# A recurrent attention with streamed weights: side transfers on another issuing engine, an output product in a bank of its own, key loads in portions, and three streaming places for 11 blocks

## The chip, the cores and the metric

The kernel runs on one core of one Trainium2 chip. The metric is the device time of one execution in microseconds, as the median of several runs; lower is better. The profile is of one further execution, and its spans are counted from its first instruction.

## The reference

Two independent computations whose outputs stand side by side.

A is a recurrent attention. The sequence of 2048 rows is cut into 64 segments of 32 rows. Each segment is put behind 8 memory rows, and the first 8 rows of its result are the memory of the next:

```python
for s in range(n_seg):                        # 64, one after the other
    xs = x[:, s * seg_len:(s + 1) * seg_len, :].copy()
    h = jnp.concatenate([mem, xs], axis=1)    # 8 + 32 rows of 1024
    q = jnp.einsum('btd,dhe->bhte', h, Wq)    # 32 heads of 128; k and v alike
    ...
    scores = jnp.where(mask[None, None], scores, -1000000000.0)
    p = _softmax(scores, axis=-1)
    o = jnp.einsum('bhqk,bhke->bhqe', p, v)
    o = jnp.einsum('bhte,hed->btd', o, Wo)
    mem = o[:, :M, :].copy()
    outs.append(o[:, M:, :])
```

B is a long convolution: from complex parameters a kernel K of 1024 channels by 2048 steps, which is convolved with u by Fourier transforms, plus `u * Dskip`.

## The kernel before

**Order of the whole.** Part B runs first (`part_b`, from line 639), part A after it (`part_a`, from line 233). Work of A that doesn't hang on the memory (projections of the last 8 rows of each segment, line 115) is woven into B. The order of the instructions on each engine is that of the program, written by hand; a tile's dependencies become semaphore waits. SyncE issues nearly all transfers, in the order of the program: one that waits holds up all behind it.

**B's end: spectra.** The loop on lines 1301 to 1345 has 16 passes, b = 0 to 15: four quarters of the channels, four blocks of frequencies each. In pass b, TensorE makes the spectrum of the keys for pass b + 1 (line 1039), VectorE multiplies pass b's with that of u (`pointwise`, lines 1210 to 1224; the first multiply by u is line 1218), and SyncE loads u's for pass b + 2 (`load_u`, two transfers on line 1013). From b = 4 on two inverse transforms follow in each pass (`inverses`). In pass 0, line 1306 issues the key loads of the third and fourth quarter: `load_k` (line 978) makes 31 small transfers for a quarter, all on SyncE. They are used from pass 7 on, and negated on ScalarE at the end of pass 6 (line 1336). In passes 0 to 3 SyncE also loads eight inverse matrices (line 1325), and weights of A where room has come free (`residents`, from line 1408).

**A's loop: segments.** All weights of A are cut into blocks of 128 x 2048 (512 KB): eight for each of k, q and v in two halves t of the heads, and 16 of the output projection. Here k1.4 is block 4 of k in half 1, and o11 the output's block 11. Most blocks stay in SBUF. Three are kept in PSUM, as bits (`KEPT`: k0.7, q0.7 or half of it, half of o15), and come into SBUF in each segment by `fetch` (line 311, copies on VectorE, line 292). Twelve are streamed from DRAM in each segment. `unit(key)` returns a block; for a streamed one `stage` (line 294) issues its load into the next of four places in turn (`SLOTS`). As SyncE runs ahead of TensorE, a load goes out when TensorE has done with the block that was in its place, four streamed blocks before.

A segment runs on TensorE as k0, q0, k1, q1, v0, v1 (`quads`: eight blocks each, four matmuls of 32 x 512 a block, line 364), with transposes (line 375), scores (lines 389 and 393) and products (lines 433 and 437) between them, and then the 16 blocks of the output projection (`oproj`, line 463). k0 is transposed by way of the copies KT0 (VectorE) and q0 by way of QT0 (ScalarE, line 483).

**Side transfers**, all on SyncE: `load_pk` (128 KB, the last rows' keys and queries of the segment, line 327), `load_vx` (their values and the next rows of x, 112 KB, line 333) and `stores` (two of 64 KB, lines 343 and 347, for the segment before). They are hung in front of the load of a certain streamed block by `between`. Small tiles of a segment lie by hand in one arena (`AT`, byte offsets), so a load waits until what was at its place has been read.

**A segment's end** (lines 565 to 577). The projection ends in bank b3, in the half `pp[:, 1]`. VectorE copies its left half out (line 568), ScalarE then the right half (line 569). The product of the last rows with half 1 (`pv_l`: four matmuls with V1 and one with the rows' own values) goes to `pp[:, 0]`, in the same bank b3, behind them. Then two transposes (line 574) and a copy on VectorE (line 575) put the memory rows into hT, which the next segment's first matmul waits for. The last segment also has GpSimd sort results for the closing output projection (line 603).

Of the kernel before, what the change touches and what calls it, by code (L numbers as in the profile page):

```python
# [21 lines left out]

STREAM = {("k", 0): (0, 6), ("q", 0): (3,), ("k", 1): (2,), ("q", 1): (0, 5), ("v", 0): (3, 7), ("v", 1): (4,)}
STREAM_O = (1, 7, 12)

BANK = {("k", 0): "b0", ("q", 0): "b1", ("k", 1): "b2", ("q", 1): "b0", ("v", 0): "b3", ("v", 1): "b2"}
KEPT = {("k", 0, 7): (("K7a", 0, 512), ("K7b", 512, 512), ("K7c", 1024, 512), ("K7d", 1536, 384), (None, 1920, 128)),
        ("q", 0, 7): (("Q7a", 1024, 512), ("Q7b", 1536, 512)),  # L30
        ("o", 15): (("Oa", 1024, 512), ("Ob", 1536, 384), (None, 1920, 128))}
HALF = (("q", 0, 7), ("o", 15))
SLOTS = 4

ARENA = 5984
AT = {"K7a": 2048, "K7b": 4960, "K7c": 0, "K7d": 3168, "ob": 1024, "pk": 3936, "vx": 0, "Q7a": 4960, "Q7b": 0, "k0": 2048,
# [196 lines left out]
def part_a(ctx, tc, x, src, WD, HE, seg_len, out_a, ahead, W_res, rest, places, first):  # L233
# [66 lines left out]
    def load_kept(key):  # L300
        t_ = first.pop(key) if key in first else stage(key, src(key))
        kept[key] = {}
        for n in (1,) if key in HALF else (0, 1):
            kept[key][n] = ps_k.tile([128, 512], F32, name="keep", tag="keep%d" % sum(len(b) for b in kept.values()))
            words(kept[key][n][:], t_[:, 1024 * n:1024 * n + 1024])
        if key in HALF:
            t_ = ahead.low["half"] if key[0] == "q" else wres.tile([128, 1024], BF16, name="Whalf")
            nc.sync.dma_start(out=t_[:], in_=src(key)[:, 0, :] if key[0] == "o" else src(key)[:, 0:1024])
            halves[key] = [(0, 1024, t_)]
# [14 lines left out]

    def load_pk(j):
        pk = at("pk", 512)
        nc.sync.dma_start(out=pk, in_=PKd[j])
        return pk

    def load_vx(j):  # L330
        n = 448 if j + 1 < NS else 256
        vx = at("vx", 448)
        nc.sync.dma_start(out=vx[:, 0:n], in_=VXd[j + 1, :, 0:n])
        return vx

    def put_xt(vx):
# [3 lines left out]
        return ap.to_broadcast(shape)  # L340

    def stores(s, ob):
        nc.sync.dma_start(out=OLd[s // 8][:, 256 * (s % 8):256 * (s % 8) + 256], in_=ob[:, 1, :])
        rows = out_a[s * SL:s * SL + SL, :].rearrange("r (q d) -> q r d", q=4)
        if s + 1 < NS:

            nc.sync.dma_start(out=rows, in_=ob[:, 0, :])
        else:
            for q in range(4):
                nc.sync.dma_start(out=rows[q][0:XM], in_=ob[32 * q:32 * q + XM, 0, :])  # L350

    load_kept(("k", 0, 7))
    fetch(("k", 0, 7))
    between["q", 0, 3] = lambda: load_kept(("q", 0, 7))
    between["v", 0, 3] = lambda: load_kept(("o", 15))
    for s in range(NS):
        def quads(m, t, kcs, a=None):
            if a is None:
# [69 lines left out]
            spread_l(nc.gpsimd, L[:, 1], lt[:, 4, 0:XL], 0, 16, XL)  # L428
            return L

        def pv(p, t, V, pb, lbs, first=True):
            for hl in range(4):
                nc.tensor.matmul(p[:, hl, :], lhsT=V[:, 128 * hl:128 * hl + 128], rhs=pb[:, hl, :],  # L433
                                 start=(first and hl == 0), stop=False, skip_group_check=True)
            p, lo = p.rearrange("p a b -> p (a b)"), 0
            for lb in lbs:
                nc.tensor.matmul(p[:, lo:lo + lb.shape[1]], lhsT=vl[:, t, :], rhs=lb,  # L437
                                 start=False, stop=True, skip_group_check=True)
                lo += lb.shape[1]
# [9 lines left out]
            nc.scalar.copy(out=o, in_=p[:].rearrange("p a (g q) -> p a g q", g=4))  # L449
            return o  # L450

        def pv_l(pl_, t, V, L):

            pv(pl_[:, t], t, V, L[:, 0].rearrange("p (a b) k -> p a (b k)", a=4), [L[:, 1].rearrange("p a k -> p (a k)")], first=(t == 0))

        def oproj(po, us, oT):
            for u in us:
# [5 lines left out]
                            nc.tensor.matmul(po[32 * qt:32 * qt + 32, o_:o_ + rhs.shape[1]], lhsT=oT[:, h % 4, (h % 16) // 4, :], rhs=rhs,  # L463
                                             start=False, stop=(h == 31), tile_position=(0, 32 * qt), skip_group_check=True)

        pks, vxs = [], []
        between["k", 1, 2] = lambda: pks.append(load_pk(s))
        if s:
            between["q", 1, 0] = lambda: stores(s - 1, ob)
        between["v", 0, 7] = lambda: vxs.append(load_vx(s))  # L470
        a = quads("k", 0, range(KC))
        k0 = evac(a, "k0")
        a = quads("q", 0, range(0, 6))
# [3 lines left out]
        sc0 = new_sc("b1")  # L477
        a = quads("k", 1, range(0, 3))
        pq, pk_ = (ps.tile([128, 4, 4, SL], BF16, name="tr", tag=tag) for tag in ("b0", "b3"))
        tr(q0, pq)  # L480
        tr(k0, pk_)
        QT0, KT0 = at("QT0", 4, 4, SL), at("KT0", 4, 4, NK)
        nc.scalar.copy(out=QT0, in_=pq[:])
        nc.vector.tensor_copy(out=KT0[:, :, :, 0:SL], in_=pk_[:])  # L484
        quads("k", 1, range(3, 6), a)
        pk = pks[0]
        kl, ql = ([pk[:, 256 * t + o:256 * t + o + 128].rearrange("p (a g k) -> p a g k", a=4, g=4) for t in range(2)] for o in (0, 128))
        put_kl(KT0, 0)
        scores(0, sc0, QT0, KT0)
# [47 lines left out]
        powers(sc1, 0)  # L537
        highest(sc1, 1)
        a = quads("v", 1, range(0, 4))
        vx = vxs[0]  # L540
        vl = vx[:, 0:256].rearrange("p (t e) -> p t e", t=2)
        pv0 = pv_x(0, V0, pb0, lb0)
        pp = ps.tile([128, 2, 256], F32, name="pp", tag="b3")
        pl_ = pp[:, 0, :].rearrange("p (t a k) -> p t a k", t=2, a=4)
        pv_l(pl_, 0, V0, L0)
        o0 = evac_o(pv0, "o0")
        pt1 = norm(sc1, 0, "pn1", "pt1")
        pb1 = at("pb1", 4, 4, SL)
# [16 lines left out]
        oproj(pp[:, 1, :], range(8, 16), o1)  # L565
        ob = at("ob", 2, 256)
        osb = ob[:, 0, :]
        nc.vector.tensor_copy(out=osb[:, 0:128], in_=pp[:, 1, 0:128])
        nc.scalar.copy(out=osb[:, 128:256], in_=pp[:, 1, 128:256])  # L569
        pv_l(pl_, 1, V1, L1)  # L570
        if s + 1 < NS:
            pt_o = ps.tile([128, 2, 4, SL], BF16, name="tro", tag="b2")
            for j in range(2):
                nc.tensor.transpose(out=pt_o[:, j, :, :].rearrange("p a b -> p (a b)"), in_=osb[:, 128 * j:128 * j + 128], identity=ident[:])
            nc.vector.tensor_copy(out=hT[:, :, XM:SL].rearrange("p (q j) r -> p j q r", j=2), in_=pt_o[:, :, :, XM:SL])
            fetch(("k", 0, 7))
        nc.scalar.copy(out=ob[:, 1, :], in_=pp[:, 0, :])

    order = sorted(range(16), key=lambda u: ("o", u) not in W_res)
    wo = {}  # L580
# [58 lines left out]
def part_b(ctx, tc, u, A_re, A_im, B_re, B_im, C_re, C_im, log_dt, Dskip, out_b, ahead, copies, residents, first_state):  # L639
# [335 lines left out]
                    at += n  # L975
            put(Kd[640:641, dsl], kx[P0:P0 + 1, NC - 1, :])

    def load_k(d0, n_d, qs, KT):
        dsl = slice(d0, d0 + n_d)

        def rows(r0, n, step=1):
            return Kd[r0:r0 + step * (n - 1) + 1:step, dsl]
        n_q = [0]

        def get(out, in_):
            qs[n_q[0] % len(qs)].dma_start(out=out, in_=in_)
            n_q[0] += 1
        for r in (0, 2, 1, 3):
            k0 = KT[:, 4 * r, :]
            get(k0[0:64], rows(r, 64, 4))  # L990
            get(k0[64:128], rows(256 + (0, 0, 1, 2)[r], 64, 2))
            k1 = KT[:, 4 * r + 1, :]
            if r == 2:
                get(k1[0:128:2], rows(384, 64, 2))
                get(k1[1:128:2], rows(386, 64, 2))
            else:
                get(k1[:], rows(384 + (0, 0, 0, 1)[r], 128))
            for mc in (2, 3):
                k2 = KT[:, 4 * r + mc, :]
                q0 = 512 + 64 * (mc - 2)  # L1000
                get(k2[0:128:2], rows(q0, 64))
                if r == 0:
                    get(k2[1:128:4], rows(q0, 32, 2))
                    get(k2[3:128:4], rows(q0 + 2, 32, 2))
                else:
                    get(k2[1:128:2], rows(q0 + 1, 64))
        return KT
# [266 lines left out]
    def inverse(dq, c, uu, neg, mn):  # L1274
# [14 lines left out]
        v.tensor_tensor(out=uu[:], in0=uu[:], in1=yb[:].rearrange("p b t s e -> p b (t s e)"), op=ALU.add)  # L1289
        gp.dma_start(out=out_v[r][:, mc:mc + 2, d], in_=uu[:])  # L1290

    todo = [(dq, c) for dq in range(4) for c in range(0, 16, 2)]
    nxt = []
    Bs = [None] * 4
# [6 lines left out]
    for b in range(16):  # L1301
        dq = b // 4
        if b % 4 == 0:
            Bs[dq] = (bp0, bp)[dq % 2].tile([128, 4, 2, 2, 2, DQ], BF16, name="Bt", tag="B")
        if b == 0:
            ks += [load_k(DQ * i, DQ, (sy,), KT2[i - 2]) for i in (2, 3)]
        if b == 3:
            nxt = [load_inverse(*todo[n_]) for n_ in range(NIV)]
            pointwise(b, *now)
            ctx_h.close()  # L1310
            ctx_p.close()
            ps_h = ctx.enter_context(tc.tile_pool(name="b_psh", bufs=3, space=PSUM))
            ps_y = ctx.enter_context(tc.tile_pool(name="b_psy", bufs=2, space=PSUM))
        if b + 1 < 16:
            s_ = [ps_h.tile([128, 2, 2, DQ], F32, name="hps", tag="h") for _ in range(2)]
            spectrum(b + 1, [halves(t_) for t_ in s_])
            then = s_[0][:], odd([halves(t_) for t_ in s_])
        if b != 3:
            pointwise(b, *now)
        now = then  # L1320
        if b + 2 < 16:
            spectra.append(load_u(b + 2))
        if b < 4:
            for i in (2 * b, 2 * b + 1):
                sy.dma_start(out=MI[i][:], in_=MId[2 * i:2 * i + 2].rearrange("c p a k q -> p c a k q"))
        for _ in range({1: 1, 2: 1, 3: 1, 6: 4, 11: 2, 12: 2, 13: 4, 14: 4}.get(b, 0)):
            next(resident)
        if b == 4:
            state = first_state(iv.tile([8, D], BF16, name="m0", bufs=1), iv.tile([128, 8, 24], BF16, name="xt0", bufs=1))
            next(state)  # L1330
        if b == 13:
            state.send(ps_y.tile([128, 8, 128], BF16, name="yp", tag="yp")[:, :, 0:8])
        if b >= 4:
            inverses(2)
        if b == 6:
            negate(ks[1:])
# [166 lines left out]
```

## Time and profile before

| | |
|---|---|
| median of 3 runs (lowest, highest) | 2226.33 us (2224.5, 2230.53) |
| profiled execution, time | 2218.38 us |
| its span | 2216.7 us |
| mean granted TensorE clock | 0.972 |
| busy: TensorE, its weight loads | 85%, 53% |
| busy: VectorE, ScalarE, GpSimd | 67%, 47%, 18% |
| DMA moved, mean over the span | 590.82 MB, 267 GB/s |
| line 577, one a segment: first and last start | 810.8 and 2156.9 us |

A line of the page's slices has forty digits, each the busy share of one fortieth of the span in tenths. Lines of a timeline give start, duration, engine, source line, operation, tiles as written <- read, shape and number, and in brackets the idle time before the first of them with what ended it. Lines of the waits give who waited for whom, the total in us, how often, and the longest. SPq is SyncE's issuing of transfers.

### The profile page before, as it was taken

To read this page: it belongs to the slowest core of one execution; us is meant where nothing else is said; L and a number is where in the kernel's file an instruction comes from. 1 tells how busy PE (TensorE), PEld (TensorE's weight loads), DVE (VectorE), ACT (ScalarE), POOL (GpSimd) and SP (SyncE) were. 2 spreads that over 40 slices of the span, in tenths; PEclk is the share of its full clock that TensorE was granted. 3 is DMA by queue.
4 is the path that set the end of the run, shared out by engine and by line. 5 is a ranking of instruction groups with operands and counts; after the bars stand their busy time and mean duration, and the time that the engine had idled before them with its cause. 6 is when DMAs were issued, how large, how long until landed. Compare 5 with 4: busy or idle time off the path is not lost.

```text
span 2216.7 us, 79278 instructions
## 1 busy us (share of the span) xinstructions
PE 1874.8 (85%) x33734; PEld 1176.4 (53%) x33734; DVE 1475.7 (67%) x3800; ACT 1041.7 (47%) x1855; POOL 404.5 (18%) x786
## 2 busy tenths in 40 slices
PE   1599999971999779898998898989989988998859
PEld 1365656651888535555555555545555455555434
DVE  8589999983999346665666666656656666666630
ACT  6699999940333224343443443443434434434420
POOL 2154453560011111111111111101111111111020
PEclk9999999976999879999999999999999999999989
DMA  6767787564536789999999999999999999999960
GB/s 160 203 193 237 213 217 201 154 167 158 194 119 209 268 321 326 308 324 316 318 327 315 324 328 311 323 319 315 329 313 321 323 313 325 325 324 325 317 247 28
DMA packets 344023, 590.82 MB, mean 267 GB/s; under 512 B 108537, under 2 KB 220185, under 8 KB 341621
## 3 DMA queue, kind: packets, MB, share of 16 engines
q1 hardware_dynamic: 331972, 547.87, 74.8%
q0 software_dynamic: 11696, 37.88, 4.9%
q8 instruction: 264, 4.33, 0.8%
q14 instruction: 91, 0.74, 0.1%
HBM read 530.86 MB, written 65.26 MB: 269 GB/s over the span
## 4 chain that ended last, share of the span: by engine, by line
PE 24%; DMA 19%; DVE 14%; issue 4%; ACT 2%; POOL 1%; SPq 0%; DVEq 0%; ACTq 0%; POOLq 0%
PE acc L364 11%; DMA wst<-WD_q 11%; PE pp L463 6%; DMA wst<-WD_v 5%; DVE arena L421 3%; PE pe L603 2%; DVE a_mx L398 2%; DVE arena L411 2%; DMA wst<-WD_k 2%; PE tr L375 1%; DVE a_mx L408 1%; ACT sc L404 1%; DVE arena L412 1%; DVE sc L401 1%; PE pv L437 1%
## 5 line engine op out<-in xcount | busy, mean ns | idle before, releaser
L364 PEld LDWEIGHTS <-a_hT 128*32 128x32 bf16 x12352 | 324.0, 96 | 378.0 <-issue 79.4
L370 ACT CAST arena<-acc 128x512 bf16<-128x512 f32 x384 | 225.3, 587 | 350.8 <-PE acc L364 296.2
L364 PE MATMUL acc<-W,a_hT 128*32 128x512 bf16 x4864 | 371.7, 382 | 0.0
L364 PE MATMUL acc<-wst,a_hT 128*32 128x512 bf16 x2304 | 231.3, 386 | 62.1 <-DMA wst<-WD_q 20.4
L463 PEld LDWEIGHTS <-arena 128*32 128x32 bf16 x8256 | 214.8, 97 | 80.4 <-issue 49.0
L292 DVE TENSOR_SCALAR arena<-keep 128x256 int32<-128x256 int32 (+1 forms) x512 | 175.6, 395 | 45.3 <-PE acc L364 41.5
L404 ACT ACTIVATE sc<-sc 128x160 f32<-128x160 f32 x256 | 73.7, 288 | 248.9 <-DVE sc L401 218.4
L463 PE MATMUL pp<-W_o,arena 128*32 128x256 bf16 x4608 | 174.2, 275 | 7.0 <-DMA W_o<-in_A_Wo_dram 6.7
L378 POOL COPY arena<-arena 128x128 bf16<-128x128 bf16 x128 | 39.1, 306 | 751.7 <-PE tr L375 462.0
L364 PE MATMUL acc<-MF,a_hT 128*32 128x512 bf16 x2048 | 158.4, 382 | 0.0
L398 DVE TENSOR_REDUCE a_mx<-sc 128x4 f32<-128x160 f32 x256 | 81.0, 316 | 109.6 <-ACT sc L404 56.0
L1039 PEld LDWEIGHTS <-MF 128*128 128x128 bf16 x1024 | 102.6, 100 | 64.3 <-issue 45.5
L1039 PE MATMUL hps<-KT,MF 128*128 128x256 bf16 x720 | 94.2, 283 | 48.7 <-DVE x L1214 45.7
L484 DVE COPY arena<-tr 128x512 bf16<-128x512 bf16 x64 | 27.2, 424 | 161.4 <-ACT sc L383 158.4
L433 PEld LDWEIGHTS <-arena 128*128 128x128 bf16 x1024 | 55.2, 97 | 138.9 <-ACT arena L569 61.6
L167 PE MATMUL pro<-xTl,wsl 128*128 128x512 bf16 x512 | 119.1, 383 | 5.2 <-ACT xTl L111 5.2
L426 POOL TENSOR_TENSOR arena<-arena,a_BD 128x128 bf16<-128x128 bf16 x128 | 51.0, 398 | 355.5 <-DVE arena L413 314.7
L408 DVE TENSOR_REDUCE a_mx<-sc 128x4 f32<-128x160 f32 x256 | 82.0, 320 | 50.4 <-ACT sc L404 50.4
L412 DVE STREAM_TRANSPOSE arena<-arena 128x128 bf16<-128x128 bf16 x256 | 79.8, 312 | 41.2 <-PE pp L433 19.5
L1271 PE MATMUL yp<-Bt,MI 128*128 128x256 bf16 x680 | 102.8, 273 | 0.8 <-ACT yb L1287 0.8
L1077 ACT ACTIVATE E<-pa 128x648 bf16<-128x648 f32 x128 | 91.3, 713 | 17.8 <-PE pa L1069 14.1
L433 PE MATMUL pp<-arena 128*128 128x32 bf16 x512 | 33.2, 178 | 75.1 <-ACT arena L569 50.5
(319 smaller groups left out, 4052.5 us busy)
## 6 DMA issues: line engine op xcount, KB each, us to landing
wst<-WD_k SPq DMA_DIRECT2D x192, 512.0 KB
wst<-WD_q SPq DMA_DIRECT2D x192, 512.0 KB
wst<-WD_v SPq DMA_DIRECT2D x192, 512.0 KB
wst<-WD_o SPq DMA_DIRECT2D x192, 512.0 KB
Ud<-ux POOLq DMA_DIRECT2D x16, 1024.0 KB, 6.2
uq<-Ud SPq DMA_DIRECT2D x32, 512.0 KB
wsl<-in_A_Wk_dram SPq DMA_DIRECT2D x16, 512.0 KB
wsl<-in_A_Wv_dram SPq DMA_DIRECT2D x16, 512.0 KB
```

Of the source, the lines that this page charges most:

```text
L167: nc.tensor.matmul(a[:], lhsT=w[:, kc, 128 * j:128 * j + 128], rhs=xTl[:, kc, :, :].rearrange("p s k -> p (s k)"), start=(kc == 0), stop=( ...
L292: nc.vector.tensor_scalar(out=out.bitcast(I32), in0=in_.bitcast(I32), scalar1=0, scalar2=None, op0=ALU.bitwise_or)
L364: nc.tensor.matmul(a[32 * g:32 * g + 32, o_:o_ + rhs.shape[1]], lhsT=hT[:, kc, :], rhs=rhs, start=(kc == 0), stop=(kc == KC - 1), tile_pos ...
L370: nc.scalar.copy(out=q, in_=a[:])
L398: nc.vector.tensor_reduce(out=mx[:, 4 * i:4 * i + 4], in_=sc[:, i], axis=AX.X, op=ALU.max)
L404: nc.scalar.activation(out=sc[:, i], in_=sc[:, i], func=ACT.Exp, scale=scale)
L408: nc.vector.tensor_reduce(out=m_, in_=sc[:, i], axis=AX.X, op=ALU.add)
L412: nc.vector.transpose(out=pt[:, 0:4, :], in_=pn[:, :, 0:SL])
L463: nc.tensor.matmul(po[32 * qt:32 * qt + 32, o_:o_ + rhs.shape[1]], lhsT=oT[:, h % 4, (h % 16) // 4, :], rhs=rhs, start=False, stop=(h == 3 ...
L1039: pe.matmul(s_[r][half][:, cs, :], lhsT=MF[:, kc, 4 * rr + mc, cs, :], rhs=rhs, start=(i == 0 and mc == 0), stop=(i == 1 and mc == 3), ski ...
L1077: sc.activation(out=T["E", r, e // 4][:, lo:lo + 8 * NE].rearrange("p (i c) -> p i c", i=2), in_=T.pop(("p", r, e))[:, :, 0:4 * NE], func= ...
L1271: pe.matmul(yp[:, b, :], lhsT=m_[:, b, cs, kc, :], rhs=Bt[:, kc, j, half, c_, :], start=(kc == 0 and cs == 0 and half == 0), stop=(kc == 3 ...
```

## The change

- Eleven blocks are streamed in place of twelve, through three places in place of four; the block no longer streamed is resident, in the room of the fourth place. Which blocks are streamed changes.
- The side transfers are issued by ScalarE, at fixed points of a segment: VX after QT0; PK of the next segment and both stores at the segment's end.
- At the end one ScalarE copy takes the whole projection out. The second half's product for the last rows gets a bank of its own (b2), and is split: four matmuls ahead of the transposes, one behind the copy into hT. The transposes go to bank b0. The fetch of k0.7 comes behind the fifth matmul.
- k0 is transposed ahead of q0.
- The key loads of the third and fourth quarter are put on a list, from which each pass issues ten, behind its load of u's spectra.

```diff
-STREAM = {("k", 0): (0, 6), ("q", 0): (3,), ("k", 1): (2,), ("q", 1): (0, 5), ("v", 0): (3, 7), ("v", 1): (4,)}
-STREAM_O = (1, 7, 12)
+STREAM = {("k", 0): (2, 5), ("k", 1): (0, 4), ("q", 1): (2,), ("v", 0): (1, 5), ("v", 1): (3, 6)}
+STREAM_O = (4, 11)
...
-SLOTS = 4
+SLOTS = 3
...
-        nc.sync.dma_start(out=pk, in_=PKd[j])
+        nc.scalar.dma_start(out=pk, in_=PKd[j])
...
-        nc.sync.dma_start(out=vx[:, 0:n], in_=VXd[j + 1, :, 0:n])
+        nc.scalar.dma_start(out=vx[:, 0:n], in_=VXd[j + 1, :, 0:n])
...
-        nc.sync.dma_start(out=OLd[s // 8][:, 256 * (s % 8):256 * (s % 8) + 256], in_=ob[:, 1, :])
+        nc.scalar.dma_start(out=OLd[s // 8][:, 256 * (s % 8):256 * (s % 8) + 256], in_=ob[:, 1, :])
...
-            nc.sync.dma_start(out=rows, in_=ob[:, 0, :])
+            nc.scalar.dma_start(out=rows, in_=ob[:, 0, :])
...
-    between["q", 0, 3] = lambda: load_kept(("q", 0, 7))
-    between["v", 0, 3] = lambda: load_kept(("o", 15))
+    pk = load_pk(0)
+    between["k", 0, 5] = lambda: load_kept(("q", 0, 7))
+    between["v", 0, 5] = lambda: load_kept(("o", 15))
...
-        def pv_l(pl_, t, V, L):
-
-            pv(pl_[:, t], t, V, L[:, 0].rearrange("p (a b) k -> p a (b k)", a=4), [L[:, 1].rearrange("p a k -> p (a k)")], first=(t == 0))
+        def pv_l(pl, t, V, L, parts=(0, 1)):
+
+            if 0 in parts:
+                pv(pl, t, V, L[:, 0].rearrange("p (a b) k -> p a (b k)", a=4), [])
+            if 1 in parts:
+                pv(pl, t, None, None, [L[:, 1].rearrange("p a k -> p (a k)")])
...
-        pks, vxs = [], []
-        between["k", 1, 2] = lambda: pks.append(load_pk(s))
-        if s:
-            between["q", 1, 0] = lambda: stores(s - 1, ob)
-        between["v", 0, 7] = lambda: vxs.append(load_vx(s))
...
+        tr(k0, pk_)
         tr(q0, pq)
-        tr(k0, pk_)
         QT0, KT0 = at("QT0", 4, 4, SL), at("KT0", 4, 4, NK)
         nc.scalar.copy(out=QT0, in_=pq[:])
+        vx = load_vx(s)
...
-        nc.vector.tensor_copy(out=osb[:, 0:128], in_=pp[:, 1, 0:128])
-        nc.scalar.copy(out=osb[:, 128:256], in_=pp[:, 1, 128:256])
-        pv_l(pl_, 1, V1, L1)
+        nc.scalar.copy(out=osb, in_=pp[:, 1, :])
+        pl = ps.tile([128, 4, 32], F32, name="pl", tag="b2")
+        pv_l(pl[:], 1, V1, L1, (0,))
         if s + 1 < NS:
-            pt_o = ps.tile([128, 2, 4, SL], BF16, name="tro", tag="b2")
+            pt_o = ps.tile([128, 2, 4, SL], BF16, name="tro", tag="b0")
             for j in range(2):
                 nc.tensor.transpose(out=pt_o[:, j, :, :].rearrange("p a b -> p (a b)"), in_=osb[:, 128 * j:128 * j + 128], identity=ident[:])
             nc.vector.tensor_copy(out=hT[:, :, XM:SL].rearrange("p (q j) r -> p j q r", j=2), in_=pt_o[:, :, :, XM:SL])
+        pv_l(pl[:], 1, V1, L1, (1,))
+        if s + 1 < NS:
             fetch(("k", 0, 7))
-        nc.scalar.copy(out=ob[:, 1, :], in_=pp[:, 0, :])
+        nc.scalar.copy(out=ob[:, 1, 0:128], in_=pp[:, 0, 0:128])
+        if s + 1 < NS:
+            pk = load_pk(s + 1)
+        nc.scalar.copy(out=ob[:, 1, 128:256], in_=pl[:].rearrange("p a k -> p (a k)"))
+        if s + 1 < NS:
+            stores(s, ob)
...
         def get(out, in_):
-            qs[n_q[0] % len(qs)].dma_start(out=out, in_=in_)
+            q = qs[n_q[0] % len(qs)]
             n_q[0] += 1
+            if later is None:
+                q.dma_start(out=out, in_=in_)
+            else:
+                later.append(lambda: q.dma_start(out=out, in_=in_))
...
-            ks += [load_k(DQ * i, DQ, (sy,), KT2[i - 2]) for i in (2, 3)]
+            ks += [load_k(DQ * i, DQ, (sy,), KT2[i - 2], keys) for i in (2, 3)]
...
         if b + 2 < 16:
             spectra.append(load_u(b + 2))
+        for _ in range(min(10, len(keys))):
+            keys.pop(0)()
```

More of the change, by code (lines that the diff above doesn't have):

```diff
@@ L342, in stores @@
     def stores(s, ob):
-        nc.sync.dma_start(out=OLd[s // 8][:, 256 * (s % 8):256 * (s % 8) + 256], in_=ob[:, 1, :])
+        nc.scalar.dma_start(out=OLd[s // 8][:, 256 * (s % 8):256 * (s % 8) + 256], in_=ob[:, 1, :])
         rows = out_a[s * SL:s * SL + SL, :].rearrange("r (q d) -> q r d", q=4)
         if s + 1 < NS:
-            nc.sync.dma_start(out=rows, in_=ob[:, 0, :])
+            nc.scalar.dma_start(out=rows, in_=ob[:, 0, :])
         else:
             for q in range(4):
-                nc.sync.dma_start(out=rows[q][0:XM], in_=ob[32 * q:32 * q + XM, 0, :])
+                nc.scalar.dma_start(out=rows[q][0:XM], in_=ob[32 * q:32 * q + XM, 0, :])
     load_kept(("k", 0, 7))
     fetch(("k", 0, 7))
-    between["q", 0, 3] = lambda: load_kept(("q", 0, 7))
-    between["v", 0, 3] = lambda: load_kept(("o", 15))
+    pk = load_pk(0)
+    between["k", 0, 5] = lambda: load_kept(("q", 0, 7))
+    between["v", 0, 5] = lambda: load_kept(("o", 15))
     for s in range(NS):
@@ L429, in left_blocks, with pv @@
             return L
-        def pv(p, t, V, pb, lbs, first=True):
-            for hl in range(4):
+        def pv(p, t, V, pb, lbs):
+            for hl in range(4 if V is not None else 0):
                 nc.tensor.matmul(p[:, hl, :], lhsT=V[:, 128 * hl:128 * hl + 128], rhs=pb[:, hl, :],
-                                 start=(first and hl == 0), stop=False, skip_group_check=True)
+                                 start=(hl == 0), stop=False, skip_group_check=True)
             p, lo = p.rearrange("p a b -> p (a b)"), 0
@@ L479, in part_a @@
         pq, pk_ = (ps.tile([128, 4, 4, SL], BF16, name="tr", tag=tag) for tag in ("b0", "b3"))
+        tr(k0, pk_)
         tr(q0, pq)
-        tr(k0, pk_)
         QT0, KT0 = at("QT0", 4, 4, SL), at("KT0", 4, 4, NK)
         nc.scalar.copy(out=QT0, in_=pq[:])
+        vx = load_vx(s)
         nc.vector.tensor_copy(out=KT0[:, :, :, 0:SL], in_=pk_[:])
         quads("k", 1, range(3, 6), a)
-        pk = pks[0]
         kl, ql = ([pk[:, 256 * t + o:256 * t + o + 128].rearrange("p (a g k) -> p a g k", a=4, g=4) for t in range(2)] for o in (0, 128))
@@ L539, in part_a @@
         a = quads("v", 1, range(0, 4))
-        vx = vxs[0]
         vl = vx[:, 0:256].rearrange("p (t e) -> p t e", t=2)
@@ L543, in part_a @@
         pp = ps.tile([128, 2, 256], F32, name="pp", tag="b3")
-        pl_ = pp[:, 0, :].rearrange("p (t a k) -> p t a k", t=2, a=4)
-        pv_l(pl_, 0, V0, L0)
+        pv_l(pp[:, 0, 0:128].rearrange("p (a k) -> p a k", a=4), 0, V0, L0)
         o0 = evac_o(pv0, "o0")
@@ L976, in put_values, with load_k @@
             put(Kd[640:641, dsl], kx[P0:P0 + 1, NC - 1, :])
-    def load_k(d0, n_d, qs, KT):
+    def load_k(d0, n_d, qs, KT, later=None):
         dsl = slice(d0, d0 + n_d)
@@ L1290, in inverse @@
         gp.dma_start(out=out_v[r][:, mc:mc + 2, d], in_=uu[:])
+    keys = []
     todo = [(dq, c) for dq in range(4) for c in range(0, 16, 2)]
```

## The prediction

> **What bounds the kernel now.** I read the page's slices first, to find the stages.
>
> ```profile
> PE   1599999971999779898998898989989988998859
> DMA  6767787564536789999999999999999999999960
> ```
>
> Two places matter: the dip of TensorE in slices 9 and 10 (about 500 to 560 us), and the long stretch from slice 14 on, the 64 segments, where the transfers are at 9 throughout. The dip, from VectorE's and SyncE's timelines (start, duration, engine, line, tiles, idle before):
>
> ```profile
> 503.14 1.22 DVE L1214 TENSOR_TENSOR x<-hps,osb__7465 128x1024 f32<-128x1024 f32 x1
> 539.63 1.23 DVE L1218 TENSOR_TENSOR y<-uq,x 128x1024 f32<-128x1024 f32 x1 [35.27 <-DMA uq<-Ud]
> ```
> ```profile
> 495.81 39.11 SPq L986 DMA_DIRECT2D KT<-Kd  x62
> 535.02 1.00 SPq L1013 DMA_DIRECT2D uq<-Ud  x2
> ```
>
> VectorE stands 35.27 us for one pair of spectra, which SyncE issues at 535.02 because 62 key loads of 0.63 us each stand in front of it.
>
> The segments: the starts of the copy on line 577 give 62 intervals of 21.02 us in the mean, the shortest 20.45 (repeatedly, so with no stall), and a last one of 42.99 in which TensorE waits 20.99 us for GpSimd's copies. TensorE's timeline round one segment's end:
>
> ```profile
> 1504.02 0.22 PE L463 MATMUL pp<-a_S,arena 128*32 128x128 bf16 x1
> 1505.03 0.27 PE L433 MATMUL pp<-arena 128*128 128x32 bf16 x4 [0.79 <-ACT arena L569]
> 1505.14 0.22 PE L437 MATMUL pp<-arena 128*128 128x128 bf16 x1
> 1505.20 0.27 PE L574 MATMUL tro<-a_ident,arena 128*128 128x128 bf16 x2
> 1505.75 0.40 PE L364 MATMUL acc<-wst,a_hT 128*32 128x512 bf16 x4 [0.28 <-DVE a_hT L575]
> ...
> 1513.00 0.40 PE L364 MATMUL acc<-wst,a_hT 128*32 128x512 bf16 x4 [0.68 <-DMA wst<-WD_q]
> ```
>
> and SyncE's, the issue of the block that TensorE waits for at 1513.00:
>
> ```profile
> 1506.81 1.00 SPq L297 DMA_DIRECT2D wst<-WD_q  x2
> ```
>
> So 6.2 us from issue to use. SyncE's waits in 1200 to 1500 us (14 segments; total, times, longest):
>
> ```profile
> SPq L297 <- PE acc L364: 73.8, 91, 2.2
> SPq L327 <- POOL arena L421: 17.6, 14, 1.3
> SPq L343 <- ACT arena L577: 10.3, 12, 0.9
> SPq L333 <- PE acc L364: 9.0, 14, 1.2
> SPq L347 <- DVE arena L292: 8.3, 14, 0.9
> ```
>
> The first line says that a load starts when a place comes free; the other four, 45.2/14 = 3.2 us a segment, that side transfers hold up the loads behind them. Summed over 57 segments, TensorE's gaps that end with a streamed block are 0.58 us a segment, which is the whole distance from 20.45 to 21.02. In 1500 to 1521 us the packets ran at up to 410 GB/s, counted in fifths of a microsecond, with dips after 1503 and 1505, while SyncE stood at the side transfers: the mean of 320 is not its ceiling. A loss here comes from when a load is issued and how long it takes.
>
> **What the Trainium skill says.** "DMA: Bandwidth & Descriptors", section Anatomy of one DMA, fits 2.0 us plus bytes/436e3 (measured on GpSimd's path): 3.2 us for 512 KB. The trace's landing semaphores show more: with no side transfer near and over 2 us since the load before, medians of 4.61 and 4.62 us (blocks k0.0 and q0.3; 5% to 95% 3.9 to 5.7). I use the trace. The same page, section Issuing engines are not separate DMA queues: issuing from several engines saves only issue time, the 16 movers are shared. So I move the side transfers' bytes, and don't remove them; no run here shows two issuing engines at once in this stage. "PSUM — Partial Sum Buffer", section PSUM bank collisions raise a hardware error: engines must be kept apart by bank and quadrant. That agrees with the 0.79 us: the product writes the bank that both evictions read.
>
> **The change, part by part.**
>
> *Key loads in portions.* The pair that lands late is now issued behind only the skip vector, at 495.8. Before it took 4.6 us from issue to use (535.02 to 539.63); so it is there at 500.4, and VectorE wants it at 504.4. All 35.3 us go. Next late? A pass is VectorE's, 12.0 us (490.01 to 502.01); SyncE per pass has 1.0 for two spectra, 10 x 0.63 of keys, 0.94 and 0.36 for matrices and weights: 8.6. It keeps up. The last two keys are issued some 598 on the old clock, landed about 601; their negation on ScalarE starts at 602.76. Gain 35.3; bounds 28 (a later pair still late by half a pass) and 36.
>
> *End of a segment.* Before, from the last projection matmul's end (1504.24) to the next segment (1505.75): 1.51. Now one ScalarE copy of 128x256 (0.37, line 577's size) replaces 0.29 on VectorE, then 0.27 on ScalarE: 0.09 + 0.37 + 0.06 = 0.52 against 0.79, 0.27 saved. The first four products go into that pause, the fifth into the 0.28 pause: another 0.17 (1505.03 to 1505.20). Together 0.43. The K fetch stays behind the hT copy on VectorE, as before. Transposing k0 ahead of q0 removes a wait for q0's eviction, 0.09 in the mean, and makes QT0 later by four transposes; its slack was 0.26 (2120.23 to 2120.49). I take 0.05. The stall-free segment becomes 20.45 - 0.48 = 19.97.
>
> *Issues on ScalarE.* Four a segment, 0.32, 0.32, 0.56 and up to 0.57. At the end ScalarE does 0.09 + 0.37 + 0.27 + 0.35 + 0.27 + 0.1 + 0.32 + 0.56 = 2.3 us after the last matmul; the next eviction (k0) is ready 1.08 + 1.74 = 2.8 after it. The VX issue stands before an exponential that waits 1.6 us anyway. Cost 0; if the stores waited, up to 0.3 a segment. SyncE loses its 3.2 us of standing.
>
> *Three places, 11 blocks.* This decides. A block must be issued, land and be used in the time between the use of the third block before it and its own. Overhead: TensorE's matmuls start, 0.43 later SyncE issues (1507.06, 1507.49); landing to TensorE 0.05 (1512.95, 1513.00). So the window needed is the landing time + 0.48; with 4.6, 5.1. The windows of the new placing, from the starts in TensorE's timeline (a kc of q, k or v is 0.217, transposes 0.55 and 0.71, products 1.34 and 0.81) and 19.97:
>
> ```
> use of:   k0.2  k0.5  k1.0  k1.4  q1.2  v0.1  v0.5  v1.3  v1.6  o4    o11
> at us     0.43  1.09  3.64  5.38  6.97  8.48  10.20 11.75 13.88 15.18 17.83
> window    6.52  5.88  5.78  4.95  5.88  4.84  4.82  4.78  5.40  4.98  6.08
> ```
>
> A stall widens the windows across it. k1.4 is issued at 0.86, beside the PK load and the two stores (before, medians of 5.14 for k1.2 beside the PK load and 5.55 for q1.0 behind the stores), so 5.1 + 0.48 = 5.58: stall 0.63. v0.1 then has 5.47, enough. v0.5 needs 5.1 and 0.1 to 0.2 for VX: stall 0.3 to 0.4. v1.3 has 5.1, o4 5.0: 0.1 together. Sum 1.1. Landings spread by over 0.5 either way and early ones earn nothing; as my estimate that adds 0.1, since k1.4 already covers the next windows. Total 1.2: 19.97 + 1.2 = 21.15, against 21.02: +0.13 x 62 = +8 us. The faster segment and the missing block are eaten by the missing place. Bounds: landing in 4.2 (the fastest twentieth): k1.4 alone stalls, some 0.3, segment 20.3; landing in 4.8: 0.83 + 0.5 + 0.3 + 0.3 spread = 1.9, segment 21.9.
>
> *Once each.* The first segment takes its weights at 1.35 us a block with TensorE waiting for each (from 797.86 on); one more block is resident and loaded there: +1.4. After the last segment the output projection no longer waits 0.79 + 0.17: -0.9.
>
> **Sum.** -35.3 + 8 + 1.4 - 0.9 = -26.8. The profiled execution took 2218.4 us (span 2216.7 and 1.7 around it): 2191.6. It lay 8 us under the median of the runs, 2226.3; against that 2199.5, so 2200.
>
> **Rivals.**
> (1) Places don't bind: with side transfers out of SyncE's queue loads are issued evenly and land in 4.2. For: the dips of the mover fall where SyncE stands, and landings of 6 to 6.6 (v0.3, v0.7) are queueing behind bursts. Against: 4.6 is measured with hardly a queue. Segment 20.2: -0.8 x 62 = -50, total -85: 2140.
> (2) Slower: the three places bind harder, at the first block after a segment's start (k1.4) and the v blocks. With 4.8 to 4.9, 21.9: +0.88 x 62 = +55, total +20: 2246. It decides from 21.58 on, where 0.56 x 62 equals the 35 us of the keys, at a landing time of about 4.7. For: a load with its predecessors still under way took 4.7 in the median. Against: fewer loads are under way at once.
> (3) ScalarE's issues wait and hold up k0's eviction, 0.3 x 62 = 19 us: 2219, no change. For: two issues wait for ScalarE's own copies. Against: 0.5 us of room.
> (4) The keys' gain is lost to another late transfer, half of it: 2217.
>
> **How the numbers follow.** Chances: forecast 0.40 (its own range 2170 to 2222), (1) 0.25, (2) 0.24, (3) 0.06, (4) 0.05. A measurement of this kernel can't tell under 0.3%, 6.7 us, from no change. Faster: 0.36 of the forecast, 0.25 and 0.02 of (3) and (4): 0.63. Same: 0.04 of it, 0.04 of (2), 0.06: 0.14. Slower: 0.20 of (2) and 0.03: 0.23. The range leaves out the far tenth at each end: 2135 to 2246.
>
> **What would show it.** No gap of tens of us on VectorE before the first multiply of the third pass. L571's transposes 0.5 us after the last projection matmul. TensorE's waits for WD_k at k1.4 as the largest DMA wait, 0.5 us or more a segment, then WD_v; SyncE waiting only for TensorE. If the shortest segment isn't near 20.0, the end's gain is wrong; if DMA waits are under 0.4 a segment, rival (1); over 1.7, rival (2).

## The result and the profile after

| | before | after |
|---|---|---|
| median of 12 runs | 2223.97 us | 2223.46 us |
| ratio, 95% interval | | 1.0003 (0.9982 to 1.0023) |
| profiled execution, time | 2218.38 us | 2223.77 us |
| a segment, mean of the 60 between the second and the last two | 21.00 us | 21.52 us |
| of that, TensorE waiting for streamed blocks | 0.57 us | 1.85 us |
| first segment's copy (lines 569 and 565) starts | 810.0 us | 777.6 us |

No change that can be measured, where the forecast was 2200 us. The last line and the fourth say why: part A starts 32 us earlier, and its segments give the 32 us back. The slices of the page after:

```profile
PE   1599999878998589888889898888898898898859
DMA  6767776567556878888888888888888888888860
```

The 1 of TensorE's slice 10 is gone; from slice 15 on the transfers show 8 where they stood at 9, and TensorE shows mostly 8 where it stood at 8 and 9 by turns. Neither is busier than before: they wait for each other.

VectorE and SyncE where the 35 us gap was, after the change (timelines):

```profile
502.90 1.21 DVE L1222 TENSOR_TENSOR x<-hps,osb__7411 128x1024 f32<-128x1024 f32 x1
504.03 1.21 DVE L1226 TENSOR_TENSOR y<-uq,x 128x1024 f32<-128x1024 f32 x1
505.28 1.23 DVE L1227 TENSOR_TENSOR x<-uq,x 128x1024 f32<-128x1024 f32 x1
```
```profile
494.93 0.83 SPq L1021 DMA_DIRECT2D uq<-Ud  x2
496.18 8.19 SPq L995 DMA_DIRECT2D KT<-Kd  x10
504.74 0.89 SPq L1336 DMA_DIRECT2D MI<-MId  x2
505.74 0.87 SPq L1021 DMA_DIRECT2D uq<-Ud  x2
```

The spectra go out ahead of ten key loads, and the first multiply by u (line 1226 now) starts at 504.03 with no idle time ahead of it. A key load takes 0.82 us in this portion, not 0.63; SyncE still keeps up.

TensorE at one segment's end and at the next k1.4, after the change, and under it SyncE's issue of that k1.4:

```profile
1535.81 0.22 PE L467 MATMUL pp<-a_S,arena 128*32 128x128 bf16 x1
1535.96 0.27 PE L434 MATMUL pl<-arena 128*128 128x32 bf16 x4
1536.60 0.29 PE L571 MATMUL tro<-a_ident,arena 128*128 128x128 bf16 x2 [0.37 <-ACT arena L565]
1536.72 0.22 PE L438 MATMUL pl<-arena 128*128 128x128 bf16 x1
1537.16 0.61 PE L365 MATMUL acc<-Wlow,a_hT 128*32 128x512 bf16 x8 [0.23 <-DVE a_hT L572]
...
1544.28 0.40 PE L365 MATMUL acc<-wst,a_hT 128*32 128x512 bf16 x4 [1.95 <-DMA wst<-WD_k]
```
```profile
1538.04 0.32 SPq L297 DMA_DIRECT2D wst<-WD_k  x1
```

From the last projection matmul's end (1536.03) to the next segment (1537.16) are 1.13 us, where 1.51 stood before: the new end works. But k1.4, issued as soon as k0.2's matmuls (from 1537.61) had left its place, lands 6.2 us later, and TensorE stands 1.95 us: one of the longer waits for this block, whose mean stands in the table below. TensorE's waits in 1200 to 1500 us (14 segments; total, times, longest):

```profile
PE acc L365 <- DMA wst<-WD_v: 11.2, 17, 1.4
PE acc L365 <- DMA wst<-WD_k: 8.3, 10, 2.2
PE pp L467 <- DMA wst<-WD_o: 6.7, 10, 1.1
PE tro L571 <- ACT arena L565: 5.1, 14, 0.4
```

Three of the four largest are streamed blocks. By block, over 55 or 56 segments, with the landing times (from a load's issue to its landing) from the trace's landing semaphores:

```
                        k0.5  k1.0  k1.4  q1.2  v0.1  v0.5  v1.3  v1.6  o4    o11   sum
waits, us a segment     0.06  0.01  0.65  0.09  0.11  0.30  0.22  0.10  0.28  0.03  1.85
share of segments       9%    4%    68%   21%   16%   45%   51%   25%   54%   11%
landing, median us      4.80  4.62  4.74  5.73  4.79  4.84  4.94  4.97  4.69  4.67
```

### The profile page after: what moved, and what is told of

It reads as the page before. It is cut to its first block, busy times and chain, and to the rows that moved or that the text cites. A ratio compares the mean times of both kernels' runs of the same rounds, so it can differ in the third digit from the quotient of the medians.

```text
span 2222.1 us, 79115 instructions
## 1 busy us (share of the span) xinstructions
PE 1881.8 (85%) x33709; PEld 1189.5 (54%) x33734; DVE 1459.4 (66%) x3736; ACT 1056.6 (48%) x1919; POOL 406.6 (18%) x786
## 4 chain that ended last, share of the span: by engine, by line
DMA 34%; PE 26%; DVE 2%; issue 2%; ACT 1%; POOL 1%; SPq 0%; ACTq 0%; DVEq 0%; POOLq 0%
DMA wst<-WD_v 12%; PE acc L365 12%; DMA wst<-WD_k 10%; PE pp L467 9%; DMA wst<-WD_o 8%; DMA wst<-WD_q 3%; PE pe L607 2%; DMA W_o<-in_A_Wo_dram 1%; ACT arena L565 1%; PE pv L434 1%; PE tro L571 1%; PE pv L438 1%; PE tr L376 1%; DVE a_hT L572 1%; DMA arena<-VXd 0%
## 5 line engine op out<-in xcount | busy, mean ns | idle before, releaser
L365 PE MATMUL acc<-W,a_hT 128*32 128x512 bf16 x4864 | 351.7, 386 | 0.0
L467 PE MATMUL pp<-W_o,arena 128*32 128x256 bf16 x5120 | 184.9, 277 | 7.5 <-DMA W_o<-in_A_Wo_dram 7.5
L379 POOL COPY arena<-arena 128x128 bf16<-128x128 bf16 x128 | 38.1, 298 | 777.6 <-PE tr L376 473.6
L365 PE MATMUL acc<-MF,a_hT 128*32 128x512 bf16 x2048 | 172.3, 387 | 0.0
L450 ACT CAST arena<-pv 128x512 bf16<-128x512 f32 x128 | 75.1, 587 | 66.3 <-PE pv L438 30.4
L565 ACT CAST arena<-pp 128x256 bf16<-128x256 f32 x64 | 23.8, 372 | 151.9 <-PE pp L467 151.9
```

Of the source, the lines that this page charges most:

```text
L365: nc.tensor.matmul(a[32 * g:32 * g + 32, o_:o_ + rhs.shape[1]], lhsT=hT[:, kc, :], rhs=rhs, start=(kc == 0), stop=(kc == KC - 1), tile_pos ...
```

## The experiments

My theory after these readings: keys and end gained what they should, and the three places took it back, because windows of 4.5 to 5 us lie in the middle of the spread of the landing times. Its rivals: ScalarE's side transfers cause the late landings; or the end's gain isn't there. Each ratio is to runs of the kernel before on the same chip, and differences between two kernels in us are worked out from the ratios, at 2222 us; by the intervals of the two ratios such a difference is known to 6 to 11 us. "Rest" is a segment without TensorE's waits for blocks; segments are means over the same 60.

| kernel | median us | ratio, 95% interval | segment | waits | rest |
|---|---|---|---|---|---|
| keys_only | 2189.2 | 0.9855 (0.983, 0.988) | 21.08 | 0.68 | 20.40 |
| end_keys | 2171.6 | 0.9779 (0.9745, 0.9812) | 20.80 | 0.82 | 19.98 |
| four_places | 2140.9 | 0.9644 (0.9626, 0.9663) | 20.35 | 0.35 | 20.00 |
| sides_hooked | 2244.4 | 1.0114 (1.0077, 1.0151) | 22.02 | 2.30 | 19.71 |
| three_even | 2191.4 | 0.9857 (0.9824, 0.989) | 21.19 | 1.09 | 20.09 |
| four_even | 2130.9 | 0.9595 (0.9577, 0.9613) | 20.15 | 0.29 | 19.86 |
| stores_late | 2243.9 | 1.0102 (1.0082, 1.0122) | 21.86 | 1.50 | 20.35 |
| four_eleven | 2126.1 | 0.9564 (0.9544, 0.9584) | 20.00 | 0.12 | 19.88 |
| places_only | 2291.4 | 1.031 (1.0265, 1.0356) | 21.89 | 1.73 | 20.16 |

**keys_only**: the kernel before with the diff's key loads, and nothing else.

> The kernel before with the key loads in portions and nothing else. Theory (the whole gap of 35 us on VectorE goes, and nothing after it takes its place): 2224 - 35 = 2189, segments unchanged at 21.0 us. Rival (half of it is lost to another late transfer): 2206, with a wait of 15 us or more somewhere between 500 and 750 us.

32 us (1.45%) faster; its first segment's copy starts at 777.0 instead of 810.0. The whole gap is gone and no wait of its size took its place; segments are what they were.

**end_keys**: that, and the diff's new end and order of transposes.

> The kernel before with the key portions, the new end of a segment (one copy, product in its own bank and split) and the order of k0's and q0's transposes; four places, twelve blocks and side transfers on SyncE as before. Theory as predicted (end worth 0.48 a segment, stalls as before): 2189 - 30 = 2159. If the end is worth what the changed kernel shows without its waits for blocks (20.43 - 19.67 = 0.76) and the stalls stay at 0.6 to 0.8: 2189 - 62 x 0.55 to 0.75 = 2142 to 2155. Rival (the end's gain is not there, the short intervals of the changed kernel are segments in which the gaps lie under the waits for blocks): 2185 or more.

0.9855 to 0.9779: the end is worth 17 us. The rest falls by 0.42 (20.40 to 19.98), near the predicted 0.48, and the waits grow by 0.14; a shorter segment shortens the windows, but no run shows that this is the reason. The 0.14 is 9 us over 62 segments, most of the 13 us by which the time lies over the first figure expected, 2159. The 19.67 that I had read from the changed kernel is not its stall-free segment: where TensorE waits for a block, its small waits for VectorE and GpSimd fall into that time. So the second figure in the expectation was wrong, and the rival as well.

**four_places**: the changed kernel, with this undone.

```diff
-STREAM = {("k", 0): (2, 5), ("k", 1): (0, 4), ("q", 1): (2,), ("v", 0): (1, 5), ("v", 1): (3, 6)}
-STREAM_O = (4, 11)
+STREAM = {("k", 0): (0, 6), ("q", 0): (3,), ("k", 1): (2,), ("q", 1): (0, 5), ("v", 0): (3, 7), ("v", 1): (4,)}
+STREAM_O = (1, 7, 12)
...
-SLOTS = 3
+SLOTS = 4
...
-    between["k", 0, 5] = lambda: load_kept(("q", 0, 7))
-    between["v", 0, 5] = lambda: load_kept(("o", 15))
+    between["q", 0, 3] = lambda: load_kept(("q", 0, 7))
+    between["v", 0, 3] = lambda: load_kept(("o", 15))
```

> The changed kernel, but with the four places and the twelve streamed blocks of the kernel before. In the changed kernel a segment takes 21.52 us in the mean, of which TensorE waits 1.85 for streamed blocks; 19.67 is left without these waits. Theory (three places leave windows of 4.8 to 5 us, and the spread of the landing times reaches beyond them): with windows of 5.2 to 7.4 the waits fall to 0.2 to 0.6, a segment to 19.9 to 20.3, the time to 2223 - 62 x 1.2 to 1.6 = 2120 to 2150. Rival (transfers issued by ScalarE disturb the loads, whatever the number of places): waits stay at 1.2 or more and grow with the twelfth block, a segment is 20.9 or more, the time 2180 or more.

80 us faster than the changed kernel (1.0003 to 0.9644), and 30 faster than end_keys, from which only the issuing of the side transfers divides it: the engine, and the moments in a segment. TensorE's waits in 1200 to 1500 us of four_places:

```profile
PE tro L571 <- ACT arena L565: 5.4, 15, 0.4
PE acc L365 <- DVE a_hT L572: 3.4, 15, 0.2
PE acc L365 <- DMA wst<-WD_q: 2.9, 5, 1.1
PE acc L365 <- DMA wst<-WD_k: 1.3, 2, 0.7
PE acc L365 <- DMA wst<-WD_v: 1.2, 1, 1.2
```

The streamed blocks have dropped from 27.0 us to 5.4 (one more segment end lies in the stretch), and the end's own two pauses lead. So it isn't ScalarE's issuing that makes loads late: with it waits are less than in end_keys (0.35 against 0.82), and the rest is the same (20.00 against 19.98), so that ScalarE's issues hold up nothing there.

Where the 30 us come from is seen on SyncE. Its waits for side transfers in 1200 to 1500 us of end_keys, which four_places doesn't have:

```profile
SPq L327 <- POOL arena L421: 18.0, 14, 1.6
SPq L333 <- PE acc L364: 7.5, 14, 0.6
SPq L343 <- ACT arena L582: 6.8, 12, 0.9
```

In end_keys k1.2, behind PK, is issued 1.25 us after the matmuls that free its place have started (median of 60 segments), q1.0, behind the stores, 1.14; all other blocks there, and all in four_places, at 0.43 to 0.45. TensorE's waits for k1.2, q1.0 and v0.7, the three blocks behind a side transfer, fall from 0.69 us a segment to 0.17. v0.7 was issued on time in both; its landing shortened, from 6.6 to 6.1. No run has SyncE issue the side transfers at ScalarE's moments, so the share of the engine and that of the moment stay unseparated.

**sides_hooked**: the changed kernel with the side transfers on SyncE, hung in front of streamed blocks as before.

```diff
+        between["k", 1, 4] = lambda: pks.append(load_pk(s))
+        if s:
+            between["q", 1, 2] = lambda: stores(s - 1, ob)
+        between["v", 1, 3] = lambda: vxs.append(load_vx(s))
...
```

The part not shown turns the four `nc.scalar` issues back into `nc.sync` and takes out the calls at ScalarE's points.

> The changed kernel, but with the side transfers issued by SyncE as in the kernel before: PK in front of block k1.4, the stores in front of q1.2, VX in front of v1.3. Three places, eleven blocks, new end, key portions. Theory (the places bind; the issuing engine matters little, and SyncE's standing at the side transfers delays loads a little more): waits for blocks 1.9 to 2.8 a segment, 2223 to 2280. Rival (ScalarE's side transfers beside k1.4 cause the waits): waits of 1.0 or less, 2170 or less.

25 us slower than the changed kernel; q1.2, behind the stores, waits in 98% of the segments, 0.84 us in the mean. k1.4 waits less than in the changed kernel (0.41 against 0.65), but the sum is 2.30 where the rival said 1.0 or less: it falls a second time.

**three_even**: the changed kernel with other blocks streamed; three places and eleven blocks remain.

```diff
-STREAM = {("k", 0): (2, 5), ("k", 1): (0, 4), ("q", 1): (2,), ("v", 0): (1, 5), ("v", 1): (3, 6)}
-STREAM_O = (4, 11)
+STREAM = {("k", 0): (3,), ("q", 0): (3,), ("k", 1): (1, 6), ("q", 1): (6,), ("v", 0): (2,), ("v", 1): (2, 4)}
+STREAM_O = (4, 7, 14)
...
```

The part not shown moves the two one-time loads of the kept blocks q0.7 and o15 to other blocks.

> The changed kernel with other blocks streamed, nothing else: eleven through three places as before, but spread evenly over a segment (k0.3, q0.3, k1.1, k1.6, q1.6, v0.2, v1.2, v1.4, o4, o7, o14), so that the windows are 5.3 to 5.7 us (o14: 4.9) where the changed kernel has 4.8 to 5.0 at five blocks. Theory (each block waits where landing time + 0.48 is above its window, and the median landing time is 4.6 to 5.0): waits for blocks fall from 1.85 to 0.5 to 1.0 a segment, a segment to 20.5 to 20.9, the time to 2160 to 2185. Rival (the waits come from single late landings or from the side transfers, which no placing of blocks changes): waits stay at 1.5 or more, 2205 or more.

32 us from another placing of the blocks alone. It evens out the windows, but it also puts other blocks beside the side transfers, and these two aren't separated. The waits, 1.09, lie a little over the range expected, and so does the time (2191, up to 2185 expected); the largest wait, 0.34, is k1.1's, which is now the block beside PK and the stores and lands in 5.48.

```profile
PE acc L365 <- DMA wst<-WD_k: 7.1, 12, 2.3
PE tro L571 <- ACT arena L565: 5.1, 14, 0.4
PE acc L365 <- DVE a_hT L572: 3.2, 14, 0.2
PE acc L365 <- DMA wst<-WD_v: 2.1, 5, 1.0
```

In this view (TensorE's waits of three_even, 1200 to 1500 us) the v blocks have fallen from 11.2 to 2.1; o4 and o7 are no longer among the largest.

**four_even**: the changed kernel with four places, and twelve blocks spread as evenly.

```diff
+STREAM = {("k", 0): (2,), ("q", 0): (1, 6), ("k", 1): (3,), ("q", 1): (1,), ("v", 0): (1, 3), ("v", 1): (2, 5)}
+STREAM_O = (2, 6, 12)
...
-SLOTS = 3
+SLOTS = 4
...
```

> The kernel with four places and twelve blocks and all other parts of the change, with the twelve blocks spread evenly (k0.2, q0.1, q0.6, k1.3, q1.1, v0.1, v0.3, v1.2, v1.5, o2, o6, o12): all windows 6.3 to 7.2 us where those of the four_places kernel are 5.2 to 7.4 with two loads often in one burst. Theory: waits for blocks fall from 0.35 to 0.1 or less a segment, segment 20.0 to 20.15, time 2120 to 2130. Rival (the rest of the waits is single late landings of 6 to 7 us): waits stay at 0.25 or more, 2135 or more.

2130.9 us, the fastest kernel here that leaves nothing out: 4.05% under the kernel before, and 11 us under four_places. Against three_even, where eleven blocks are spread as evenly through three places, it is 58 us. Its waits, 0.29, are nearer the rival's figure: what is left are single late landings, which wide windows don't hold off either (v1.2, with a window of some 6.5 us, waits in 22% of the segments; its landings reach 7.15 at 95%).

**stores_late**: the changed kernel with a segment's stores in the next segment, behind QT0.

```diff
         nc.scalar.copy(out=QT0, in_=pq[:])
+        if s:
+            stores(s - 1, ob)
         vx = load_vx(s)
...
         nc.scalar.copy(out=ob[:, 1, 128:256], in_=pl[:].rearrange("p a k -> p (a k)"))
-        if s + 1 < NS:
-            stores(s, ob)
```

> The changed kernel with the two stores of a segment issued by ScalarE in the next segment, behind QT0 and in front of VX, so that only the PK load stands beside k1.4's load. Theory (k1.4 waits because its window of 4.95 is under landing time + 0.48): its wait falls only from 0.65 to 0.4 to 0.5 a segment, part of which the next blocks take over: 2205 to 2222. Rival (k1.4 waits because of the stores beside it, as the prediction had it with a landing of 5.1): its wait falls to 0.2 or less, the time by 20 to 28, 2195 to 2203.

22 us slower than the changed kernel, which neither side expected. k1.4's wait did fall, from 0.65 to 0.33, so about half of it came with the stores; the other half is left with only PK beside its load. But ScalarE's and TensorE's timelines show a new wait:

```profile
1268.77 0.33 ACTq L343 DMA_DIRECT2D OLd<-arena  x1
1273.21 0.59 ACT L371 CAST arena<-acc 128x512 bf16<-128x512 f32 x1 [0.77 <-DMA OLd<-arena]
```
```profile
1273.85 0.40 PE L376 MATMUL tr<-a_ident,arena 128*128 128x128 bf16 x4 [1.04 <-ACT arena L371]
```

The store holds its room in the arena for 4.4 us after its issue; q1's eviction, written over that room (`ob` begins at byte 1024 and is 1024 long, `q1` begins at 1536), waits for it, and q1's transposes wait for the eviction: 0.46 us a segment. v0.5, now behind these stores, waits 0.52 instead of 0.30. So the end of a segment was the better of these two places for the stores.

**four_eleven**: four places with the changed kernel's own eleven blocks. Block v1.7 is left out, and v1.5 multiplied in its place.

```diff
+        key = ("v", 1, 5) if key == ("v", 1, 7) else key
...
-SLOTS = 3
+SLOTS = 4
...
```

> The changed kernel with four places in place of three and the same eleven streamed blocks. To make room, block v1.7 is not loaded, and v1.5 is used in its place (its values are left out, its matmuls are not). Theory (the missing place is the whole loss): windows rise from 4.8 to 6.5 us to 6.3 to 8, waits for blocks fall from 1.85 to 0.15 or less a segment, a segment to 20.0 to 20.15, the time to 2223 - 62 x 1.45 to 1.6 - 4 = 2120 to 2130, within 10 us of four_even with its twelve blocks: the block less was worth next to nothing. Rival (half of the waits come from the order of these blocks and the side transfers beside k1.4): 2150 or more.

As expected: the fourth place takes the waits from 1.85 to 0.12 and the time down by 97 us. Of the streamed blocks two lines are left among TensorE's waits in 1200 to 1500 us:

```profile
PE acc L366 <- DMA wst<-WD_q: 2.7, 3, 1.7
PE acc L366 <- DMA wst<-WD_v: 1.0, 1, 1.0
```

And this isn't because the loads got faster: most of the same eleven blocks land later than in the changed kernel (v1.3 in 5.6 us in the median for 4.9, o4 in 5.4 for 4.7). It is the window that counts: 6.2 to 9.0 us in the medians of the eleven blocks, where the changed kernel has 4.7 to 6.9. four_even, with a twelfth block, is 7 us slower, but its blocks are placed differently and the difference is hardly outside its interval (6 us): what a block more costs by itself isn't shown.

**places_only**: the kernel before with three places and the eleven blocks (hooks as in sides_hooked), and nothing else.

> The kernel before with three places and the eleven blocks of the changed kernel, and nothing else: side transfers on SyncE (PK in front of k1.4, stores in front of q1.2, VX in front of v1.3), old end, keys in one go. Theory (the parts add up): end_keys to sides_hooked is the same step with the new end and the key portions in place and cost 2244.4 - 2171.6 = 73; so 2222 + 65 to 75 = 2285 to 2297. Rival (the old end's longer pauses cover part of the waits): 2270 or less.

69 us slower, as expected: alone this part would have been a loss of 3%. On top of the keys and the new end (end_keys to sides_hooked) it costs 74, with the side transfers on ScalarE as well (four_places to the changed kernel) 80: between these three the price differs by no more than they are known to (6 to 11 us). So the change, taken step by step in the order of these kernels, is keys -32, end -17, side transfers on ScalarE -30, three places with eleven blocks +80.

## Why the prediction was wrong

- **Keys, right.** -35.3 was predicted; -32 was measured, -33.0 in the start of part A. The 8.6 us of SyncE's pass was counted with 0.63 a key load, and the first portion took 0.82 each. The last two key loads go out at 567.2 and 567.7, some 5 us later than the sum had them, and ScalarE waits 3.76 us before it negates them (573.41). VectorE doesn't feel it: its first multiplies by u stay 35.0 us earlier up to the last pass.
- **End of a segment, right.** 0.48 predicted, 0.42 measured in the rest; the shortest interval is 19.87 with four places, where 19.97 was predicted. The sign that I named for it, a shortest segment near 20.0, failed in the changed kernel (20.47) only because hardly a segment of it is free of waits.
- **Issues on ScalarE, cost right.** They cost nothing: the rest stays at 20.0. What they bring I had put nowhere by itself. With four places it is 30 us: loads that had landed in 6.6 us (v0.3 and v0.7, at the medians of end_keys) land in 5.9 and 6.1 (four_places), and k1.2 and q1.0 are issued some 0.8 and 0.7 us sooner. The Trainium skill's "DMA: Bandwidth & Descriptors", section Issuing engines are not separate DMA queues, says that issuing from several engines saves only the time that the sequencer takes to issue. The runs show more than that: SyncE no longer stands at a side transfer that isn't ready, with loads behind it (engine and moment were moved together).
- **Three places: the step that failed.** Mechanism and order were right: k1.4 waits most (0.63 predicted, 0.65 measured), then v0.5 (0.3 to 0.4; 0.30). That k1.4's size fits is in part luck: its landing is 4.74 in the median, not 5.1, its window 4.73, not 4.95, which leaves 0.5; late landings make up the rest. The term "Total 1.2" was too small: 1.85 a segment, 21.52 us where 21.15 stood. That is 0.37 x 60 = 22 of the 32 us by which the profiled execution missed 2191.6; of the rest, some 5 are two waits of over 2 us in the third segment, 2.6 the last segment, 1.5 part A's start. It was mis-sized in three places of the sum:
  - *v1.3 and o4*, 0.1 predicted, 0.22 + 0.28 measured. "A stall widens the windows across it" let the mean wait of one block serve the next. But waits come in half of the segments. Where neither of the two blocks ahead had waited, v1.3 waited in 62% of the segments, 0.30 us in the mean; where one had, in 29%, 0.13. For o4 the figures are 76% (0.45) and 31% (0.17), all over 60 segments. And where one had waited, v1.3's landing was later too, 5.27 in the mean for 4.61; the loads may go out closer together after a wait, but no run tests that.
  - *the windows*, taken from the kernel before with its small waits in them. In the segments where o4 waits and neither block ahead of it did, TensorE is ready for it 4.06 us after its issue in the median; with 0.43 ahead of the issue the window is 4.49, not 4.98. For k1.4 it is 4.73, not 4.95.
  - *spread*, 0.1 predicted, 0.40 measured (k0.5, k1.0, q1.2, v0.1, v1.6 and o11 together). A landing time has 5% and 95% points of 4.1 and 6.5 (k1.4); early ones earn nothing, as the text said, but it priced that with the median.
  
  The base itself, 4.6 for an undisturbed landing, was right: 4.61 at v1.3 and o4 where nothing had waited.
- **The rivals.** The second set the point from which the keys' gain is gone at a segment of 21.58. The mean of the first 62 is 21.60, so the result is its break-even, not its 2246. By the sign named for it, waits of over 1.7, it is this rival that held; the time lies halfway between its figure and the forecast. The first named 2140, and four_places took 2140.9; that is chance, as its loads land in 4.6 to 6.1 us, not in 4.2, and are waited for less because there is a place more. The third gave about the right time (2219) for the wrong reason: the rest of a segment didn't grow. The fourth is excluded by keys_only.

## What to carry to other kernels

What the number of places decided here is the time from the release of a place to the use of its next block, not bandwidth: work out the window of each block, subtract the small waits that will vanish, and compare it with the far end of the landing times, not with their median. Where the windows are near the landing time, spreading the streamed blocks evenly over the loop is free and was worth 32 us here with three places, 11 with four; one place more was worth 80 to 97, and 58 where the blocks were already spread. And when several edits are measured as one, a result of "no change" can hide a gain of 79 us and a loss of 80.

## What the runs showed of the hardware

- The same 512 KB load landed in different times by what was issued around it: in 4.6 us in the median alone, in 5.5 beside 128 KB of PK and two stores of 64 KB (k1.1 in three_even), in 5.7 behind these and another block (q1.2 in the changed kernel; 5.3 in stores_late, without the stores), and in 6.6 in a burst (v0.3 in end_keys). Side transfers don't always move the median: k1.4, issued beside the same PK and stores, took 4.7, though one load in twenty took some 6.5 or more.
- A store of 64 KB issued amid the streamed loads kept its source 4.4 us in the segment shown (1268.77 to 1273.21), about as long as a load eight times its size takes to land.
- Earlier landings and fewer bytes a second didn't mean shorter waits: the changed kernel's transfers moved some 290 GB/s in the segments, its blocks landed in medians of 4.6 to 5.7 us, and TensorE waited 1.85 us a segment; four_even moved some 333 GB/s, its blocks landed in 5.0 to 5.9, and TensorE waited 0.29.
